# Linear attention and MLP, two layers: the third tile of the first MLP block turned by VectorE instead of TensorE

## The chip, the core and the metric

The kernel runs on one core of a Trainium2 chip. The time is the device time of one execution in microseconds (us). The kernel before takes 866.81 us, the median of three runs (866.64 to 866.84).

The engines are named as the profile names them: PE is TensorE (PEld its weight loads), DVE is VectorE, ACT is ScalarE, POOL is GpSimd. SPq and ACTq are the instruction queues of SyncE and ScalarE, from which DMA transfers are issued. A transfer is issued by one queue and lands later; whoever needs the data waits for the landing.

## What is computed

Two layers over x of 2048 rows by 448 columns in float32. Each layer adds a linear attention block (16 heads of 28 columns) to x, then an MLP block (448 to 1792 and back, gelu between), each on a layer norm of x:

```python
phi = lambda t: jnp.where(t > 0, t + 1, jnp.exp(t)) + 1e-6
pq, pk = phi(q), phi(k)
kv = jnp.einsum("bhsd,bhse->bhde", pk, v)
z = jnp.einsum("bhsd->bhd", pk)
num = jnp.einsum("bhqd,bhde->bhqe", pq, kv)
den = jnp.einsum("bhqd,bhd->bhq", pq, z)[..., None] + 1e-6
o = num / den
...
x = x + _A_ref(_layernorm(x, axis=-1), A_wqkv, A_wo)
x = x + _B_ref(_layernorm(x, axis=-1), B_w1, B_b1, B_w2, B_b2)
```

## The kernel before

**Tiles and stages.** The rows are cut into 16 tiles of 128 rows, and four tiles make a block. Per layer there are three stages. `phase1` goes over the 16 tiles: it makes k and the matrix G of the attention (and q for the first nine tiles). The middle, one pass over a list of tokens, turns G into the matrices M that stand for kv times the output weights, makes the queries that are left (tiles 9 to 15), and carries block 0 up to its MLP. The last stage runs the MLP over the four blocks; behind its matmuls it prepares the next block by a plan (`behind`).

**Precision.** A matmul operand is split into a high and a low part (hi by a cast on ScalarE, lo by a subtraction, mostly on VectorE), and a product is three matmuls: hi hi, hi lo, lo hi. `qh` and `ql`, `XH` and `XL` and `Mh` and `Ml` are such pairs.

**The middle.** It is written out by hand: `ORDER` (L605) is a string of tokens for each layer, and each token puts instructions at the end of the queues of the engines concerned. Every engine works through its own queue in order and waits where an operand isn't there. The tokens that matter here, j being one of the four tiles of block 0:

- `qz` (L810): GpSimd multiplies pq by z; `qs` (L814): VectorE sums that by head, takes the reciprocal and scales pq (L818 to L823); `tq` (L826): PE turns pq; `qq` (L835): ScalarE makes `qh` and VectorE `ql`; `o` (L845): twelve matmuls of `qh` and `ql` with M, in the order qh Mh, qh Ml, ql Mh (L850 to L852) for four groups.
- `la` (L867): VectorE adds the attention's output to x (L870), takes the statistics (L207, L219, L212), and GpSimd the power -1/2 (L213, `brs`); `lb` (L873): VectorE normalises the tile (L225, `xm`).
- `tu` (L296, for tiles 0 and 1): VectorE turns the tile in squares of 32 by 32 (L301, L302) into half of a 128 x 1024 square; `st` (L305) stores the square to DRAM from SP, `sp` (L309) loads it again in four transfers, so that the columns stand on the partitions; `x` (L887, by `split_t`) makes XH and XL of it.
- `T` (L883, for tiles 2 and 3): PE turns the tile with four transposes (L262); `x` (by `split_x`, L274 and L275) splits the result. For these tiles ScalarE first copies the last 64 columns once more behind the tile (L877).
- `Q`, `Qa`: eleven matmuls that make the queries of one tile (L337). `Qv` (L558) makes their phi with two passes of ScalarE and one of VectorE (L353, L354, L356) and stores it; `Qp` (L567) does it with three passes of ScalarE and an addition on GpSimd (L572 to L575).

After the list come the first matmuls of the MLP (L924, `hp`), which take all four tiles of XH side by side as their moving operand:

```python
MIDDLE = (
    "m0 qq1 m1 ms0 qq0 m2 ms1 m3 ms2 tq2 ms3 qz3 qs3 Qv1 o0 la0 qq2 o1 tq3 lb0 tu0 la1 qq3 Qv1 ",
    "m0 qq1 Qp m1 qz3 ms0 qq0 m2 ms1 m3 ms2 tq2 ms3 Qp qs3 o0 la0 qq2 o1 tq3 lb0 tu0 la1 qq3 ",
)
ORDER = [
    "Q ld1 ld0 ld2 G qz0 qz1 gt qs1 Q Qp kv qs0 tq1 Q mask qz2 tq0 qs2 ld3 b " + m +
    "o2 lb1 tu1 st la2 Q o3 sp Qv1 lb2 la3 Q T2 lb3 Qv1 x2 pre Qa x0 x1 T3 x3 Qa Qv "
    for m in MIDDLE
]
```

Of the kernel before, what the change touches and what calls it, by code (L numbers as in the profile page):

```python
# [9 lines left out]
F32 = mybir.dt.float32  # L10
# [12 lines left out]
def linear_attn_mlp_kernel(  # L23
# [12 lines left out]
    pe, act, dve, pool, sp = nc.tensor, nc.scalar, nc.vector, nc.gpsimd, nc.sync  # L36
    x0 = x_in[0]
# [7 lines left out]
    G = 112  # L45
# [10 lines left out]
    def dram(shape, dt, name):  # L56
        return tc.dram_tile(shape, dt, name=name)
# [15 lines left out]
    def t512(tag, bufs, name, dt=F32, at=0):  # L73
        n = 576 if tag in "BF" else 512
        return work.tile([128, n], dt, name=name, tag=tag, bufs=bufs)[:, at:at + 512]
# [217 lines left out]
    def half(name):  # L293
        return work.tile([128, 1024], F32, name=name, tag="S", bufs=5)
# [8 lines left out]
                      x[:, TL:].rearrange("p (m n) -> p m n", n=32)[:, None].to_broadcast([128, 2, 2, 32]))  # L303

    def store_sq(key, h):  # L305
        d = stored[key, h] = dram([128, 1024], F32, f"sq_{'_'.join(map(str, key))}_{h}")
        sp.dma_start(d, squares.pop((key, h)))

    def spread(key, h):  # L309
        r = spreads[key, h] = half("sp")  # L310
        d = stored.pop((key, h)).rearrange("(i r) (m f) -> m r i f", i=4, m=4)
        for m in range(4):
            sp.dma_start(r[m * 32:(m + 1) * 32].rearrange("r (i f) -> r i f", i=4), d[m])

    def split_t(key, t, hi, lo, eng=dve):

        x = spreads[key, t // 2].rearrange("p (i c u n) -> p u c i n", i=4, c=4, n=32)[:, t % 2]
        h = hi.rearrange("p (c i n) -> p c i n", c=4, n=32)
        act.copy(h, x)
        eng.tensor_tensor(lo.rearrange("p (c i n) -> p c i n", c=4, n=32), x, f(h), op=OP.subtract)  # L320
# [212 lines left out]
    def stage_q(l, t, cs=range(4), tag=None):  # L533
        if tag:
            qs_[l, t] = bank(tag, 4, "psq")[:, :D]
        qs_[l, t] = proj("q", ("a", l, t // 4), t % 4, qs_.get((l, t)), cs, q_at(l, t))
        if 3 in cs:
            qo.append((l, t, qs_.pop((l, t))))
# [16 lines left out]
            else:  # L555
                qo.append((0, t, o))

    def stage_qphi(n=9):  # L558
        for _ in qo[:n]:
            l, t, o = qo.pop(0)  # L560
            if (l, t) == (0, 0):
                by_rs(o)

            e = phi(o, "eq", tag="e" if t < NT - 2 else "E")
            sp.dma_start(pq_d[l][t * 128:(t + 1) * 128, :], e)

    def fill_qphi():  # L567

        l, t, o = qo.pop(0)
        e = t512("e", 3, "eq")[:, :D]  # L570
        p = t512("E", 2, "ep")[:, :D]
        act.activation(e, o, AF.Relu, scale=-1.0)  # L572
        act.activation(p, o, AF.Relu)
        act.activation(e, e, AF.Exp, scale=-1.0)
        pool.tensor_tensor(e, p, e, op=OP.add)  # L575
        sp.dma_start(pq_d[l][t * 128:(t + 1) * 128, :], e)

    def stage_g(l, t, acc, mid=lambda: None):
        h, lo = split.pop((l, t))
        kh, kl = ks.pop((l, t))  # L580
        first, last = t == 0, t == NT - 1
        x = [h[:, c * 128:(c + 1) * 128] for c in range(3)] + [h[:, TL:]]
        his = [(c, x[c], k) for c in range(4) for k in (kh, kl)]
        if t == NT - 3:
            his = his[::2] + his[1::2]
        los = [(c, lo[:, c * 128:(c + 1) * 128], kh) for c in range(3)]
        made = merge(his, los, g_at(l, t))
        for i, (c, w, k) in enumerate(made):
            if i == 3:
                mid()  # L590
            others = [m[0] for m in made[:i]], [m[0] for m in made[i + 1:]]
            pe.matmul(acc[c], w, k, start=first and c not in others[0], stop=last and c not in others[1])  # L592
# [5 lines left out]

    MIDDLE = (
        "m0 qq1 m1 ms0 qq0 m2 ms1 m3 ms2 tq2 ms3 qz3 qs3 Qv1 o0 la0 qq2 o1 tq3 lb0 tu0 la1 qq3 Qv1 ",
        "m0 qq1 Qp m1 qz3 ms0 qq0 m2 ms1 m3 ms2 tq2 ms3 Qp qs3 o0 la0 qq2 o1 tq3 lb0 tu0 la1 qq3 ",
    )
    ORDER = [  # L605
        "Q ld1 ld0 ld2 G qz0 qz1 gt qs1 Q Qp kv qs0 tq1 Q mask qz2 tq0 qs2 ld3 b " + m +
        "o2 lb1 tu1 st la2 Q o3 sp Qv1 lb2 la3 Q T2 lb3 Qv1 x2 pre Qa x0 x1 T3 x3 Qa Qv "
        for m in MIDDLE
    ]
    DEFER = NT - sum(tok in ("Q", "Qa") for tok in ORDER[0].split())  # L610

    STEP = "qp K T X s a kp n kh kl tu G bg Q ld sp"
# [260 lines left out]
    def o_n(l, b, j):  # L873
        t = b * 4 + j
        xn = xns["m", l, t] = ln_norm(sts.pop(("m", l, t)), f"xm{l}_{t}")
        if b == 0 and j >= 2:
            act.copy(xn[:, D:], xn[:, TL:D])  # L877

    def add_bias(l, b, j):
# [3 lines left out]
    def m_transpose(l, b, j):  # L883
        xn = xns.pop(("m", l, b * 4 + j))
        transpose_x(xn, xn[:, TL:], ("m", l, b), j)

    def m_split(l, b, j):  # L887

        if j < 2:
            split_t(("m", l, b), j, *block(("m", l, b)).pieces(j))  # L890
        else:
            split_x(("m", l, b), j)
# [175 lines left out]
    for l in range(LAYERS):  # L1068
        tr = SimpleNamespace(mp={})
        za, acc = phase1(l, tr)  # L1070
        if l == 0:
            background(0)
        fill = list(range(DEFER, NT))

        def biases(j):
            if l == 0:
                sp.dma_start(b1s, b1.rearrange("(c p) -> p c", p=128))
                sp.dma_start(b2b, b2[None, :].to_broadcast([128, D]))

        def pre(j):  # L1080
            for k in range(4):
                load_pq(l, 1, k)
            if l == 0:
                background(2)

        tok_ = SimpleNamespace(
            Q=lambda j: stage_q(l, fill.pop(0)), Qp=lambda j: fill_qphi(), Qv=lambda j: stage_qphi(j or 9),
            Qa=lambda j: stage_q(l, fill.pop(0), tag="acc"), G=lambda j: stage_g(l, NT - 1, acc, lambda: trans_z(tr, zs[l])),
            ld=lambda j: (load_pq(l, 0, j), load_x(l, j)), gt=lambda j: trans_gt(tr, acc),
            kv=lambda j: trans_kv(tr), mask=lambda j: trans_mask(tr), m=lambda j: trans_m(tr, j),  # L1090
            ms=lambda j: trans_ms(tr, j), qz=lambda j: q_z(l, 0, j, tr), qs=lambda j: q_scale(l, 0, j, tr),
            tq=lambda j: q_transpose(l, 0, j), qq=lambda j: q_split(l, 0, j), o=lambda j: o_mm(l, 0, j, tr),
            la=lambda j: o_ln(l, 0, j), lb=lambda j: o_n(l, 0, j), T=lambda j: m_transpose(l, 0, j),
            x=lambda j: m_split(l, 0, j), tu=lambda j: turn(xns.pop(("m", l, j)), ("m", l, 0), j),
            st=lambda j: store_sq(("m", l, 0), 0), sp=lambda j: spread(("m", l, 0), 0), pre=pre, b=biases)
        for tok in ORDER[l].split():
            name, j = tok.rstrip("0123456789"), int("0" + tok.lstrip("abcdefghijklmnopqrstuvwxyzQTG"))
            getattr(tok_, name)(j)
        assert not fill and not qo
        table(AF.Gelu_apprx_tanh)  # L1100
        q_z(l, 1, 0, tr)
        mlp1(l, 0, 0)
        trans_chunks(tr)
        for b in range(NB):
            acc = [bank("acc", 4, f"y{j}")[:, :D] for j in range(4)]
            nxt = b + 1 < NB
            if not nxt and l + 1 < LAYERS:
                st_k = stage_square(wqkv[:, D:2 * D])
                st_q = stage_square(wqkv[:, :D])
                load_to(l + 1, PRE - 1)  # L1110
            for i in range(NF):
                if i + 1 < NF:
                    mlp1(l, b, i + 1)
                elif nxt:
                    mlp1(l, b + 1, 0)
                if l == 0 and b == 0 and i:
                    background(1, 1)
                if i == NF - 2 and not nxt and l + 1 < LAYERS:
                    table(AF.Exp)
                if 9 <= i < 13:  # L1120
                    add_bias(l, b, i - 9)
                if nxt:
                    behind(l, b, i, tr)
                elif l + 1 < LAYERS:
                    if i == 2:
                        split_kq("k", st_k)
                    if i == 5:
                        split_kq("q", st_q)
                    if i in (3, 4, 6, 7, 8):
                        t = (3, 4, 6, 7, 8).index(i)  # L1130
                        stage_a(l + 1, t)
# [35 lines left out]
```

## Time and profile before

| | us |
|---|---|
| median of three runs | 866.81 |
| the profiled execution | 866.72 |
| its span, first to last instruction | 865.0 |
| busy in the span: PE, PEld, DVE | 860.0, 770.6, 494.6 |
| busy in the span: ACT, POOL | 346.5, 211.1 |

The span is 1.72 us shorter than the execution's time. The granted TensorE clock is full in all 40 slices of the page. Times in the views below are counted from the start of the span. The middle of layer 0 lies at about 104 to 135 us, that of layer 1 at about 530 to 561 us. A row of the timeline has the start, the time from first start to last end, the engine, the line, the operation with what it writes and reads, the shape, and how many such instructions follow each other.

### The profile page before, as it was taken

To read this page: it belongs to the slowest core of one execution; us is meant where nothing else is said; L and a number is where in the kernel's file an instruction comes from. 1 tells how busy PE (TensorE), PEld (TensorE's weight loads), DVE (VectorE), ACT (ScalarE), POOL (GpSimd) and SP (SyncE) were. 2 spreads that over 40 slices of the span, in tenths; PEclk is the share of its full clock that TensorE was granted. 3 is DMA by queue.
4 is the path that set the end of the run, shared out by engine and by line. 5 is a ranking of instruction groups with operands and counts; after the bars stand their busy time and mean duration, and the time that the engine had idled before them with its cause. 6 is when DMAs were issued, how large, how long until landed. Compare 5 with 4: busy or idle time off the path is not lost.

```text
span 865.0 us, 11662 instructions
## 1 busy us (share of the span) xinstructions
PE 860.0 (99%) x4181; PEld 770.6 (89%) x4181; DVE 494.6 (57%) x966; ACT 346.5 (40%) x606; POOL 211.1 (24%) x243
## 2 busy tenths in 40 slices
PE   9999999999999999999999999999999999999998
PEld 8999988888888888888899998988888888888887
DVE  7888596559456443236477876864674383533112
ACT  7776635333323322333356565433232233233231
POOL 3665612235013012012222343120220140140000
PEclk9999999999999999999999999999999999999999
DMA  5385536533313402051145433252332413111001
GB/s 171 128 248 174 183 90 216 183 112 108 134 61 117 147 0 98 1 182 49 49 152 185 163 130 108 103 187 80 117 109 88 139 72 112 50 49 43 0 1 43
DMA packets 63642, 94.76 MB, mean 110 GB/s; under 512 B 8928, under 2 KB 58720, under 8 KB 63584
## 3 DMA queue, kind: packets, MB, share of 16 engines
q1 hardware_dynamic: 63408, 93.87, 33.0%
q8 instruction: 33, 0.54, 0.3%
q14 instruction: 25, 0.20, 0.1%
q10 hardware_dynamic: 176, 0.14, 0.0%
HBM read 56.17 MB, written 34.60 MB: 105 GB/s over the span
## 4 chain that ended last, share of the span: by engine, by line
PE 99%; DVE 0%; issue 0%; ACT 0%; DVEq 0%
PE hp L924 32%; PE y L954 10%; PE y L953 10%; PE y L955 10%; PE G L592 8%; PE psq L337 8%; PE psk L337 8%; PE op L862 2%; PE op L861 2%; PE op L863 2%; PE op L851 1%; PE op L850 1%; PE op L852 1%; PE kvp L759 1%; PE mp L769 1%; PE psk L551 1%
## 5 line engine op out<-in xcount | busy, mean ns | idle before, releaser
L930 DVE TENSOR_TENSOR gl<-g,gh 128x512 fp32r<-128x512 f32 x112 | 83.2, 743 | 293.8 <-ACT gh L929 293.8
L926 ACT ACTIVATE g<-hp,b1s 128x512 f32<-128x512 f32 x112 | 77.4, 691 | 399.6 <-PE hp L924 398.8
L954 PE MATMUL y<-w2l,gh 128*128 128x448 f32 x447 | 163.6, 366 | 0.0
L953 PE MATMUL y<-w2h,gh 128*128 128x448 f32 x447 | 162.0, 362 | 0.0
L955 PE MATMUL y<-w2h,gl 128*128 128x448 f32 x447 | 160.1, 358 | 0.0
L924 PE MATMUL hp<-XH,w1h 128*128 128x512 f32 x336 | 130.7, 389 | 0.0
L924 PE MATMUL hp<-XH,w1l 128*128 128x512 f32 x336 | 130.7, 389 | 0.0
L924 PE MATMUL hp<-XL,w1h 128*128 128x512 f32 x336 | 130.1, 389 | 0.0
L213 POOL TENSOR_TENSOR brs<-bve,mhalf 128x1 f32<-128x1 f32 x63 | 39.3, 623 | 286.0 <-DVE bve L212 285.5
L953 PEld LDWEIGHTS y<-w2h,gh 128*128 128x128 f32 x447 | 83.7, 187 | 9.4
L954 PEld LDWEIGHTS y<-w2l,gh 128*128 128x128 f32 x447 | 83.9, 188 | 7.0
L955 PEld LDWEIGHTS y<-w2h,gl 128*128 128x128 f32 x447 | 84.0, 188 | 5.2 <-DVE gl L930 0.2
L924 PEld LDWEIGHTS hp<-XL,w1h 128*128 128x128 f32 x336 | 63.1, 188 | 13.1
L924 PEld LDWEIGHTS hp<-XH,w1h 128*128 128x128 f32 x336 | 63.0, 187 | 10.7
L924 PEld LDWEIGHTS hp<-XH,w1l 128*128 128x128 f32 x336 | 63.1, 188 | 9.9
L929 ACT CAST gh<-g 128x512 fp32r<-128x512 f32 x112 | 70.1, 626 | 3.5
L337 PE MATMUL psk<-wk,XH 128*128 128x448 f32 x210 | 61.8, 364 | 0.0
L337 PE MATMUL psq<-wq,XH 128*128 128x448 f32 x210 | 61.3, 366 | 0.0
L812 POOL TENSOR_TENSOR pz<-pq,zb 128x448 f32<-128x448 f32 x32 | 36.9, 1154 | 90.5 <-DVE dn L818 59.1
L462 POOL TENSOR_TENSOR xnl<-x,xnh 128x384 fp32r<-128x384 f32 x32 | 34.8, 1088 | 70.0 <-ACT xnh L461 56.7
L592 PE MATMUL G<-kh,xnh 128*128 128x448 f32 x128 | 46.8, 368 | 0.0
L592 PE MATMUL G<-kl,xnh 128*128 128x448 f32 x128 | 46.0, 365 | 0.0
(161 smaller groups left out, 1481.7 us busy)
## 6 DMA issues: line engine op xcount, KB each, us to landing
x<-in_A_x_dram SPq DMA_DIRECT2D x32, 224.0 KB, 3.7
pq_d<-eq SPq DMA_DIRECT2D x32, 224.0 KB, 2.7
pq<-pq_d SPq DMA_DIRECT2D x32, 224.0 KB, 3.2
sq_m<-sq SPq DMA_DIRECT2D x14, 512.0 KB, 2.8
sp<-sq_m SPq DMA_DIRECT2D x56, 128.0 KB, 2.8
x<-x_d SPq DMA_DIRECT2D x32, 224.0 KB, 3.5
sq_a<-sq SPq DMA_DIRECT2D x12, 512.0 KB, 2.9
sp<-sq_a SPq DMA_DIRECT2D x48, 128.0 KB, 2.8
```

What stands on the lines that cost most here:

```text
L213: pool.tensor_tensor(rs, ve, mhalf, op=OP.pow)
L337: pe.matmul(o, x, p, start=(i == 0), stop=(i == 10))
L462: pool.tensor_tensor(lo[:, :TL], xn[:, :TL], f(h[:, :TL]), op=OP.subtract)
L592: pe.matmul(acc[c], w, k, start=first and c not in others[0], stop=last and c not in others[1])
L812: pool.tensor_tensor(pz, pqt[l, b * 4 + j], tr.zb, op=OP.mult)
L924: pe.matmul(o, w, r, start=(k == 0), stop=(k == len(made) - 1))
L926: act.activation(g, hp, AF.Gelu_apprx_tanh, bias=b1s[:, i:i + 1])
L929: act.copy(gh, g)
L930: dve.tensor_sub(gl, g, f(gh))
L953: pe.matmul(acc[j], gh[:, s], w2h[:, i], start=first, stop=False)
L954: pe.matmul(acc[j], gh[:, s], w2l[:, i], start=False, stop=False)
L955: pe.matmul(acc[j], gl[:, s], w2h[:, i], start=False, stop=stop)
```

## The change

- The third tile (j = 2) of block 0's layer norm is turned by VectorE too (`turn_one`), into a half square of 128 x 512 in a buffer of tag A; it is stored by a transfer of its own (`st1`) and loaded by four (`sp1`). Its four PE transposes (`T2`) and its copy of the last columns are gone.
- The loads of both squares (`sp0`, `sp1`) are issued by SP and ScalarE in turn, two each, and stand behind both stores.
- `qz1` comes ahead of `qz0`.
- In layer 0 the phi of tiles 10 and 11 goes from `Qv` to `Qp` (ScalarE and GpSimd), behind `qs3` and `qq2`; in layer 1, where these were `Qp` already, they move to the same places.
- The outputs `o2` and `o3` stand next to each other; the queries of tile 12, which stood between them, follow. `la1` and `qq3` come ahead of `tu0`.
- The phi of tiles 12 and 13 is made by `Qh` without its store; `Qw` stores both after `x3`.

```diff
     def store_sq(key, h):
-        d = stored[key, h] = dram([128, 1024], F32, f"sq_{'_'.join(map(str, key))}_{h}")
-        sp.dma_start(d, squares.pop((key, h)))
-
-    def spread(key, h):
-        r = spreads[key, h] = half("sp")
-        d = stored.pop((key, h)).rearrange("(i r) (m f) -> m r i f", i=4, m=4)
+        sq = squares.pop((key, h))
+        d = stored[key, h] = dram(list(sq.shape), F32, f"sq_{'_'.join(map(str, key))}_{h}")
+        sp.dma_start(d, sq)
+
+    def spread(key, h, queues=(sp,)):
+        d = stored.pop((key, h))
+        r = spreads[key, h] = half("sp") if d.shape[1] == 1024 else t512("A", 2, "sp")
+        d = d.rearrange("(i r) (m f) -> m r i f", i=4, m=4)
         for m in range(4):
-            sp.dma_start(r[m * 32:(m + 1) * 32].rearrange("r (i f) -> r i f", i=4), d[m])
+            eng = queues[m % len(queues)]
+            eng.dma_start(r[m * 32:(m + 1) * 32].rearrange("r (i f) -> r i f", i=4), d[m])
+
+    def turn_one(x, key):
+        sq = squares[key, 1] = t512("A", 2, "sq")
+        sq = sq.rearrange("p (m c n) -> p c m n", m=4, c=4, n=32)
+        dve.transpose(sq[:, :3], x[:, :TL].rearrange("p (c m n) -> p c m n", c=3, n=32))
+        dve.transpose(sq[:, 3].rearrange("p (u m) n -> p u m n", u=2),
+                      x[:, TL:D].rearrange("p (m n) -> p m n", n=32)[:, None].to_broadcast([128, 2, 2, 32]))
...
-    def stage_qphi(n=9):
+    held = []
+
+    def stage_qphi(n=9, hold=False):
...
-            sp.dma_start(pq_d[l][t * 128:(t + 1) * 128, :], e)
+            held.append((pq_d[l][t * 128:(t + 1) * 128, :], e))
+            if not hold:
+                store_held()
+
+    def store_held():
+        while held:
+            sp.dma_start(*held.pop(0))
...
-    MIDDLE = (
-        "m0 qq1 m1 ms0 qq0 m2 ms1 m3 ms2 tq2 ms3 qz3 qs3 Qv1 o0 la0 qq2 o1 tq3 lb0 tu0 la1 qq3 Qv1 ",
-        "m0 qq1 Qp m1 qz3 ms0 qq0 m2 ms1 m3 ms2 tq2 ms3 Qp qs3 o0 la0 qq2 o1 tq3 lb0 tu0 la1 qq3 ",
-    )
     ORDER = [
-        "Q ld1 ld0 ld2 G qz0 qz1 gt qs1 Q Qp kv qs0 tq1 Q mask qz2 tq0 qs2 ld3 b " + m +
-        "o2 lb1 tu1 st la2 Q o3 sp Qv1 lb2 la3 Q T2 lb3 Qv1 x2 pre Qa x0 x1 T3 x3 Qa Qv "
-        for m in MIDDLE
-    ]
+        "Q ld1 ld0 ld2 G qz1 qz0 gt qs1 Q Qp kv qs0 tq1 Q mask qz2 tq0 qs2 ld3 b "
+        "m0 qq1 m1 ms0 qq0 m2 ms1 m3 ms2 tq2 ms3 qz3 qs3 Qp o0 la0 qq2 Qp o1 tq3 lb0 la1 qq3 tu0 "
+        "o2 lb1 la2 tu1 st0 o3 lb2 tu2 st1 la3 Q Qh Q sp0 sp1 lb3 Qh Qa x0 x1 x2 T3 x3 Qw pre Qa Qv "
+    ] * LAYERS
...
-        if b == 0 and j >= 2:
+        if b == 0 and j == 3:
             act.copy(xn[:, D:], xn[:, TL:D])
...
-        if j < 2:
+        if j < 3:
             split_t(("m", l, b), j, *block(("m", l, b)).pieces(j))
```

More of the change, by code (lines that the diff above doesn't have):

```diff
@@ L305, in store_sq @@
     def store_sq(key, h):
-        d = stored[key, h] = dram([128, 1024], F32, f"sq_{'_'.join(map(str, key))}_{h}")
-        sp.dma_start(d, squares.pop((key, h)))
-    def spread(key, h):
-        r = spreads[key, h] = half("sp")
-        d = stored.pop((key, h)).rearrange("(i r) (m f) -> m r i f", i=4, m=4)
-        for m in range(4):
-            sp.dma_start(r[m * 32:(m + 1) * 32].rearrange("r (i f) -> r i f", i=4), d[m])
-    def split_t(key, t, hi, lo, eng=dve):
-        x = spreads[key, t // 2].rearrange("p (i c u n) -> p u c i n", i=4, c=4, n=32)[:, t % 2]
+        sq = squares.pop((key, h))
[5 more added lines that the diff above has]
+        d = d.rearrange("(i r) (m f) -> m r i f", i=4, m=4)
+        for m in range(4):
+            eng = queues[m % len(queues)]
[6 more added lines that the diff above has]
+                      x[:, TL:D].rearrange("p (m n) -> p m n", n=32)[:, None].to_broadcast([128, 2, 2, 32]))
+    def split_t(key, t, hi, lo, eng=dve):
+        x = spreads[key, t // 2]
+        if x.shape[1] == 512:
+            x = x.rearrange("p (i c n) -> p c i n", i=4, c=4)
+        else:
+            x = x.rearrange("p (i c u n) -> p u c i n", i=4, c=4, n=32)[:, t % 2]
         h = hi.rearrange("p (c i n) -> p c i n", c=4, n=32)
@@ L885, in m_transpose, with turn_xm @@
         transpose_x(xn, xn[:, TL:], ("m", l, b), j)
+    def turn_xm(l, j):
+        xn = xns.pop(("m", l, j))
+        if j < 2:
+            turn(xn, ("m", l, 0), j)
+        else:
+            turn_one(xn, ("m", l, 0))
     def m_split(l, b, j):
-        if j < 2:
+        if j < 3:
             split_t(("m", l, b), j, *block(("m", l, b)).pieces(j))
@@ L1087, in linear_attn_mlp_kernel @@
             Q=lambda j: stage_q(l, fill.pop(0)), Qp=lambda j: fill_qphi(), Qv=lambda j: stage_qphi(j or 9),
+            Qh=lambda j: stage_qphi(1, True), Qw=lambda j: store_held(),
             Qa=lambda j: stage_q(l, fill.pop(0), tag="acc"), G=lambda j: stage_g(l, NT - 1, acc, lambda: trans_z(tr, zs[l])),
@@ L1093, in linear_attn_mlp_kernel @@
             la=lambda j: o_ln(l, 0, j), lb=lambda j: o_n(l, 0, j), T=lambda j: m_transpose(l, 0, j),
-            x=lambda j: m_split(l, 0, j), tu=lambda j: turn(xns.pop(("m", l, j)), ("m", l, 0), j),
-            st=lambda j: store_sq(("m", l, 0), 0), sp=lambda j: spread(("m", l, 0), 0), pre=pre, b=biases)
+            x=lambda j: m_split(l, 0, j), tu=lambda j: turn_xm(l, j),
+            st=lambda j: store_sq(("m", l, 0), j), sp=lambda j: spread(("m", l, 0), j, (sp, act)), pre=pre, b=biases)
         for tok in ORDER[l].split():
```

## The prediction

> **What bounds the kernel now.** I read the page first, then PE's waits, then the two middles by stretch.
>
> ```profile
> PE 860.0 (99%) x4181; PEld 770.6 (89%) x4181; DVE 494.6 (57%) x966; ACT 346.5 (40%) x606; POOL 211.1 (24%) x243
> ...
> PE 99%; DVE 0%; issue 0%; ACT 0%; DVEq 0%
> ...
> PE warm L170 <- DVE one L164: 1.1, 1, 1.1
> PE psk L551 <- ACT wk L137: 0.3, 1, 0.3
> ...
> 108.00:135.14 27.14, 27.14 (x144) 23.84 (x143) 23.93 (x53) 11.25 (x23) 4.49 (x6) 1.00 0.36 108
> 533.50:560.63 27.13, 27.13 (x145) 23.70 (x143) 22.86 (x48) 12.09 (x26) 6.40 (x8) 1.00 0.29 100
> ```
>
> PE is busy for 860.0 of 865.0 us, the chain of waits is PE for 99% of the span, and the view of who waited for whom has 1.4 us for PE in all, at the launch. So the end moves by what the change takes from PE's queue and by every wait that it puts in front of PE. The last two rows are the middles of the two layers by stretch (time; busy time of PE, PEld, DVE, ACT, POOL; clock; DMA). PE has no gap there, and VectorE is busy for 23.9 of 27.1 us and 22.9 of 27.1 us, in a stage with few gaps. Whether PE keeps going is decided by how early VectorE delivers.
>
> **What is removed from PE.** `T2`, four transposes per layer.
>
> ```profile
> 129.41 0.57 PE L337 MATMUL psq<-wq,XL 128*128 128x448 f32 x2
> 129.82 0.60 PE L262 MATMUL tp<-ident,xm 128*128 128x128 f32 x4
> 130.18 0.45 PE L337 MATMUL psq<-wq,XL 128*128 128x448 f32 x1
> 130.46 0.57 PE L337 MATMUL psq<-wq,XH 128*128 128x448 f32 x2
> ...
> 438.22 2.21 PE psq L337 x11
> ```
>
> From 129.41 to 130.46 PE starts three matmuls and the four transposes in 1.05 us. Eleven such matmuls take 2.21 us, 0.20 each, so three are 0.60 and the transposes cost 0.45 us. This is on the path: -0.45 us per layer, -0.9 us in all. That is the whole of what can be gained; nothing else leaves PE's queue.
>
> **What is moved next to PE: `o3` behind `o2`.** PE weight loads carry the waits. I work in layer 1, because its middle had the GpSimd phi behind `qs3` already.
>
> ```profile
> 545.89 0.19 PEld L850 LDWEIGHTS op<-Mh,qh 112*128 112x128 f32 x1
> 546.31 0.19 PEld L852 LDWEIGHTS op<-Mh,ql 112*128 112x128 f32 x1
> 548.24 0.79 PEld L337 LDWEIGHTS psq<-wq,XH 128*128 128x128 f32 x4
> ...
> 545.58 0.68 DVE L840 TENSOR_TENSOR ql<-tq,qh 112x512 fp32r<-112x512 f32 x1
> 546.32 0.51 DVE L225 TENSOR_SCALAR xm<-x,bmv,brs 128x448 f32<-128x448 f32 x1
> 546.87 0.58 DVE L301 STREAM_TRANSPOSE sq<-xm 128x384 f32<-128x384 f32 x1
> ...
> 547.56 0.59 DVE L870 TENSOR_TENSOR x<-op,x 128x448 f32<-128x448 f32 x1
> ...
> 549.13 0.68 DVE L840 TENSOR_TENSOR ql<-tq,qh 112x512 fp32r<-112x512 f32 x1
> ```
>
> `ql` of tile 2 ends at 545.58 + 0.68 = 546.26, and `o2` loads it at 546.31: already tight. Behind `o2` come the queries of tile 12, whose weight load starts at 548.24, four in 0.79 us. With `o3` there instead, its third load, the first of `ql`, is due at 548.24 + 0.40 = 548.64. Before, `ql` of tile 3 ended at 549.13 + 0.68 = 549.81, harmless since `o3` came eleven matmuls later. Now it has to come 1.17 us earlier or PE stands, with all of PE's queue behind it.
>
> VectorE's queue in between is, in the changed program: `xm` of tile 0, then x of tile 1 with its statistics, then this `ql`; the two transposes of tile 0 (0.69 us from 546.87 to 547.56 in the present order) come after it. If `xm` takes its usual 0.51 us, the next starts 0.43 us after it (553.44 to 553.87, below), x of tile 1 at 546.75, and `ql` ends 0.81 us earlier than before, at 549.00: PE stands for 0.38 us with the wake-up of 0.02. But GpSimd now has an addition (`Qp`) queued right behind `brs`:
>
> ```profile
> 542.42 1.16 POOL L575 TENSOR_TENSOR eq<-ep,eq 128x448 f32<-128x448 f32 x1 [3.37 <-ACT eq L574]
> 542.71 1.34 DVE L823 SCALAR_TENSOR_TENSOR pq<-pq,rd 128x448 f32<-128x448 f32 x1
> 117.27 0.63 DVE L823 SCALAR_TENSOR_TENSOR pq<-pq,rd 128x448 f32<-128x448 f32 x1
> ...
> 414.84 0.55 POOL L213 TENSOR_TENSOR brs<-bve,mhalf 128x1 f32<-128x1 f32 x1 [4.34 <-DVE bve L212]
> 415.36 2.42 POOL L881 TENSOR_TENSOR x<-x,b2b 128x448 f32<-128x448 f32 x2
> 415.43 1.33 DVE L426 TENSOR_SCALAR x<-x,bmv,brs 128x448 f32<-128x448 f32 x1 [0.73 <-POOL brs L213]
> ```
>
> The first rows show a GpSimd addition holding VectorE's scaling of pq: 1.34 us in layer 1, where it ran just ahead, 0.63 in layer 0, where none ran. The last three are the situation that the change makes: `brs`, the next GpSimd addition 0.52 us after its start, the normalisation 0.07 us later still, and it takes 1.33 us in place of 0.51. ScalarE has the operands of tile 11's phi ready long before: the cast of `qh` for tile 2 and three passes come first, and `brs` of tile 0 starts later.
>
> ```profile
> 543.14 0.59 ACT L839 CAST qh<-tq 112x512 fp32r<-112x512 f32 x1 [0.80 <-PE op L851]
> 545.74 0.55 POOL L213 TENSOR_TENSOR brs<-bve,mhalf 128x1 f32<-128x1 f32 x1 [2.16 <-DVE bve L212]
> ```
>
> Three passes about as long as the cast end by 543.73 + 1.8 = 545.5, before `brs` at 545.74, which GpSimd's queue has ahead of the addition. I take the held value: `xm` takes 1.33, x of tile 1 starts at 547.56, just where it was, `ql` ends at 549.81, and PE stands for 549.84 - 548.64 = 1.20 us. Ends for the range: 0.38 (not held) and 1.20.
>
> The Trainium skill (SBUF — State Buffer, Who interferes with whom) says that the second of two such operations is blocked for the whole of the first. By it the normalisation at 415.43 would have begun when the first of the two additions ended, 415.36 + 1.21 = 416.57, and taken 1.65 us. The row has 1.33, so the ends overlap; the sum goes by the row, and what the rule would make of it is the last rival.
>
> Layer 0 comes to the same. There the addition behind `qs3` is new and stretches the scaling from 0.63 to 1.34 us (+0.71), while a vector pass of phi behind it, about as long, goes; VectorE's queue then stands as it does in layer 1.
>
> **What is added at the end of the stage.** Tile 2 reaches PE over DRAM now.
>
> ```profile
> 551.13 0.58 DVE L870 TENSOR_TENSOR x<-op,x 128x448 f32<-128x448 f32 x1
> 553.44 0.51 DVE L225 TENSOR_SCALAR xm<-x,bmv,brs 128x448 f32<-128x448 f32 x1
> 553.87 0.62 DVE L870 TENSOR_TENSOR x<-op,x 128x448 f32<-128x448 f32 x1
> 551.23 0.32 SPq L307 DMA_DIRECT2D sq_m<-sq  x1
> 553.90 1.74 SPq L313 DMA_DIRECT2D sp<-sq_m  x4
> 861.77 0.38 ACTq L950 DMA_DIRECT2D out_dram<-x  x1
> 558.50 1.14 ACT L319 CAST XH<-sp 128x512 fp32r<-128x512 f32 x2
> 559.55 0.58 ACT L274 CAST XH<-tp 128x512 fp32r<-128x512 f32 x1
> 560.43 0.19 PEld L924 LDWEIGHTS hp<-XH,w1h 128*128 128x128 f32 x1
> 134.29 0.58 ACT L274 CAST XH<-tp 128x512 fp32r<-128x512 f32 x1
> 134.95 0.19 PEld L924 LDWEIGHTS hp<-XH,w1h 128*128 128x128 f32 x1
> ...
> x_d<-x SPq DMA_DIRECT2D x16, 224.0 KB, 2.0
> DMA to landing us min/median/max: 2.5/2.8/4.4
> ```
>
> The first MLP load stands at 560.43 and the last cast of XH ends at 560.13: 0.30 us to spare. (In layer 0 the cast ended at 134.87 with the load at 134.95.) With -0.45 and +1.20 PE comes there at 561.18.
>
> VectorE after `ql` at 549.13: `tu0` 0.60 later, 0.69 us; `xm` of tile 1, 0.43; so x of tile 2 starts at 550.85 (551.13 before). Statistics to 552.42 (1.57, as from 547.56 to 549.13), `tu1` to 553.12, `xm` of tile 2, `tu2` ending at 554.52. The first store goes at 553.24 and lands 2.67 us later (551.23 to 553.90 above), 555.91. The second, 256 KB, goes at 554.54; 224 KB took 2.0 us, 512 KB 2.67, so it lands at 556.6 to 557.2; I take 556.6. ScalarE's queue waits for both landings, and behind them stand the tail copy of tile 3, the phi of tile 13 and all casts of XH. Eight loads at 0.4 to 0.5 us, four on each queue (SP took 1.74 for four, ScalarE 0.38 for one): `sp0` is issued by 556.4, `sp1` by 557.3 (or 557.9). At 2.8 us they land at 559.2 and 560.1 (560.7). Casts of tiles 0 and 1, 0.51 each, from 559.2; tile 2 at 560.2; tile 3 ends at 561.3, 0.1 us behind PE's 561.18. With the late ends: 561.8, +0.6. With earlier landings 0. I take +0.1.
>
> **At no cost.** `qz1` first lets `qs1` start one GpSimd product earlier, but PE waits for nothing there, and VectorE's next input from PE (the mask's) isn't earlier. The removed copy frees ScalarE ahead of its wait for the landings. The two extra ScalarE passes of layer 0 stand in its gaps, 0.80 us ahead of the cast at 543.14. The held stores are read again only for later blocks, and SP's queue has the loads of the next block behind them. If such a cover were gone, each would cost at most its own length, about 0.6 us.
>
> **Sum.** Per layer -0.45 + 1.20 + 0.1 = +0.85, two layers +1.7. The profiled execution took 866.72 us (its span 865.0 and 1.72 around it), 0.09 under the median: 866.72 + 1.7 = 868.4 us, +0.18% on 866.81. A change under 0.2% (1.73 us) is what a measurement here can't tell from none, so 865.08 to 868.54 counts as the same.
>
> **Rivals.**
> - VectorE isn't held (the other side, not slower). If the GpSimd addition comes after `xm` of tile 0 has started, PE stands 0.38 us and VectorE is 0.8 us earlier at the end: -0.45 + 0.38 per layer, 866.6 us; with no wait of PE at all, -0.9, 865.8 us. It decides from 0.07 us, the lead of the addition over `xm` at 415. For it: the lead is that short. Against: with that very lead it held at 415.43. 17%.
> - The square comes late. The landings ranged from 2.5 to 4.4 us; with the loads from two queues at once a last landing half-way to 4.4, 3.6 us, brings tile 2 at 560.9 and the last cast at 562.0, 0.9 us behind PE: 866.72 + 2 x 1.65 = 870.0 us. For it: ScalarE's casts now stand behind two landings in a row. Against: the four loads of 553.90 met little other traffic. 21%.
> - VectorE is held until the addition has ended: 0.3 us more per layer (1.65 in place of 1.33), 869.0 us. Against it stands the row at 415.43. 5%.
>
> **How the numbers follow.** The forecast has 57%, its own range 867.8 to 869.2, from the end wait of 0 to 0.6 per layer less small errors in the stall. A third of that lies over 868.54: 0.21, with the late square 0.21 and the whole hold 0.04 that is 0.46 slower. Same: 0.36, 0.15 of the first rival and 0.01 of the last, 0.52. Faster would need -1.73, twice what leaves PE's queue: 0.02, for what I haven't seen. The range leaves out the best case and the worst landings: 866.0 to 870.3.
>
> **What would show it.** PE's waits would have two new entries, PE `op` (its third line) for VectorE's `ql` with 1.2 us each; `xm` of tile 0 would take 1.3 us in both layers with a GpSimd `eq` starting 0.07 us ahead; the first `hp` would wait up to some tenths for ScalarE's XH. `xm` at 0.5 us in both layers, or `o3` without a wait, would make the forecast wrong; so would a first `hp` that waits over 0.6 us.

## The result, and the profile after

| | before | after |
|---|---|---|
| median of four runs, us | 866.83 (866.64 to 867.98) | 872.0 (871.33 to 872.3) |
| the profiled execution, us | 866.72 | 872.3 |
| its span, us | 865.0 | 870.6 |

The kernel is 0.57% slower: the ratio of the times is 1.0057, with a 95% interval of 1.0045 to 1.0069. That is 5.2 us where +1.7 was forecast, and outside the range of 866.0 to 870.3 us.

The page of the changed kernel and its view of who waited for whom (PE's rows; us in total, how often, the longest):

```profile
PE 860.0 (99%) x4173; PEld 769.3 (88%) x4173; DVE 500.4 (57%) x968; ACT 345.7 (40%) x606; POOL 213.5 (25%) x245
...
PE hp L949 <- ACT XH L274: 3.0, 2, 1.9
PE op L870 <- DVE ql L858: 1.9, 2, 0.9
PE warm L170 <- DVE one L164: 1.1, 1, 1.1
PE psk L565 <- ACT wk L137: 0.9, 1, 0.9
```

PE has eight instructions fewer and two new waits, each once per layer: the first MLP matmul `hp` for ScalarE's XH, and `op` of tile 3 for VectorE's `ql`. Both were named in the prediction. (These rows have the waits of the matmuls; those of the weight loads ahead of them, in the timeline below, are some 0.4 us longer.) The wait at the launch (`psk`) is 0.6 us longer than before; no edit touches the launch.

The two middles by stretch, up to the first load of `hp` (time; busy time of PE, PEld, DVE, ACT, POOL; clock; DMA share, GB/s):

```profile
108.33:137.53 29.20, 27.14 (x141) 23.10 (x139) 24.77 (x49) 11.56 (x24) 6.28 (x8) 1.00 0.44 127
536.08:565.99 29.91, 27.07 (x139) 23.02 (x138) 24.68 (x49) 11.55 (x24) 6.22 (x8) 1.00 0.39 119
```

PE stands for 2.06 and 2.84 us in a stretch that had no gap before. Now the timeline of layer 1 along the chain that ends at the first `hp`, the changed kernel:

```profile
543.17 0.19 PEld L868 LDWEIGHTS op<-Mh,qh 112*128 112x128 f32 x1
...
548.31 0.55 POOL L213 TENSOR_TENSOR brs<-bve,mhalf 128x1 f32<-128x1 f32 x1 [2.16 <-DVE bve L212]
548.83 1.16 POOL L597 TENSOR_TENSOR eq<-ep,eq 128x448 f32<-128x448 f32 x1
548.89 1.34 DVE L225 TENSOR_SCALAR xm<-x,bmv,brs 128x448 f32<-128x448 f32 x1
551.75 0.68 DVE L858 TENSOR_TENSOR ql<-tq,qh 112x512 fp32r<-112x512 f32 x1
552.49 0.19 PEld L870 LDWEIGHTS op<-Mh,ql 112*128 112x128 f32 x1 [1.30 <-DVE ql L858]
...
555.81 1.62 SPq L308 DMA_DIRECT2D sq_m<-sq  x2
558.45 1.75 SPq L316 DMA_DIRECT2D sp<-sq_m  x4
558.48 1.80 ACTq L316 DMA_DIRECT2D sp<-sq_m  x4
563.80 1.66 ACT L333 CAST XH<-sp 128x512 fp32r<-128x512 f32 x3 [2.18 <-DMA sp<-sq_m]
565.37 0.58 ACT L274 CAST XH<-tp 128x512 fp32r<-128x512 f32 x1
565.99 0.19 PEld L949 LDWEIGHTS hp<-XH,w1h 128*128 128x128 f32 x1 [2.29 <-ACT XH L274]
```

The upper part is as forecast: the GpSimd addition starts 0.06 us ahead of `xm`, `xm` takes 1.34 us, and PE waits 1.30 us for `ql`. The lower part isn't. ScalarE stands idle for 2.18 us until the first square has landed, more than 5 us after its first load was issued, and PE waits 2.29 us for the casts behind it.

The views of the tile `sp` in layer 1 give the issues (ns; first and last start in us) and the landings. First the kernel before, then the changed one:

```profile
L313 SPq DMA_DIRECT2D sp<-sq_m x4: 318/423/429, 553.9 to 555.2; - x4
DMA to landing us min/median/max: 2.5/2.8/2.9
```

```profile
L316 SPq DMA_DIRECT2D sp<-sq_m x4: 309/372/425, 558.5 to 559.8; - x4
L316 ACTq DMA_DIRECT2D sp<-sq_m x4: 342/409/453, 558.5 to 559.8; - x4
DMA to landing us min/median/max: 3.2/4.4/4.8
```

Before, each load took 2.5 to 2.9 us, the last one issued at 555.2; so the whole square of 512 KB was there 4.2 us after its first load was issued. After, the square's four loads go out within 0.4 us, and the whole square is there 5.2 us after the first. One row of the kernel before gives the frame:

```profile
540.59 0.19 PEld L850 LDWEIGHTS op<-Mh,qh 112*128 112x128 f32 x1
```

From here on times are counted from this first load of `op` of the layer (540.59 before, 543.17 after), which takes out what earlier stages add. The chain of layer 1:

| step, us after the first `op` | before | forecast | after |
|---|---|---|---|
| first store issued | 10.64 | 12.65 | 12.64 |
| first load of the first square issued | 13.31 | 15.3 | 15.28 |
| first square landed | 17.5 | 18.6 | 20.5 |
| first `hp` | 19.84 | 20.7 | 22.82 |

Layer 1 loses 2.98 us. In layer 0 the first `op` is at 115.15 before and 115.48 after, `hp` at 134.95 and 137.53: 2.25 us. With 0.33 us that the first `op` of layer 0 already comes later, that is 5.56 us, and the span grew by 5.6.

### The profile page after: what moved, and what is told of

Its sections match the earlier page's. It is cut to its first block, busy times and chain, and to the rows that moved or that the text cites. A ratio compares the mean times of both kernels' runs of the same rounds, so it can differ in the third digit from the quotient of the medians.

```text
span 870.6 us, 11660 instructions
## 1 busy us (share of the span) xinstructions
PE 860.0 (99%) x4173; PEld 769.3 (88%) x4173; DVE 500.4 (57%) x968; ACT 345.7 (40%) x606; POOL 213.5 (25%) x245
## 4 chain that ended last, share of the span: by engine, by line
PE 93%; DMA 2%; DVE 2%; issue 1%; ACT 1%; POOL 0%; ACTq 0%; SPq 0%; DVEq 0%; POOLq 0%
PE hp L949 32%; PE y L979 10%; PE y L978 10%; PE y L980 10%; PE G L614 8%; PE psk L351 8%; PE psq L351 6%; PE op L880 2%; PE op L879 2%; PE op L881 2%; DMA sp<-sq_m 1%; PE kvp L777 1%; DMA sq_m<-sq 1%; PE op L883 1%; PE op L882 1%
## 5 line engine op out<-in xcount | busy, mean ns | idle before, releaser
L334 DVE TENSOR_TENSOR XL<-sp,XH 128x512 fp32r<-128x512 f32 x54 | 45.2, 849 | 5.7 <-ACT XH L333 4.3
```

## The experiments

Each was timed in five rounds against the kernel before on the same chip, which took 866.78 to 866.95 us there (medians); the 872.0 us of the changed kernel are from its own timing, beside 866.83. Counted from the first `op` of the layer, `hp` is 19.80 and 19.84 us before, 22.05 and 22.82 after.

### One queue for the loads

```diff
-            st=lambda j: store_sq(("m", l, 0), j), sp=lambda j: spread(("m", l, 0), j, (sp, act)), pre=pre, b=biases)
+            st=lambda j: store_sq(("m", l, 0), j), sp=lambda j: spread(("m", l, 0), j, (sp,)), pre=pre, b=biases)
```

> Edit: both squares are loaded from SP alone, as the single square was before; all else as in the changed kernel (872.0 us). Theory A (volume: the last load of a square lands about 4.2 to 4.5 us after the first was issued, whichever queues issue them, since the 16 DMA engines carry the packets one after the other): the first square lands about where it did (135.0 to 135.3 in layer 0, 563.2 to 563.6 in layer 1), the second later, as SP issues its loads 0.9 us later (136.6 to 137.0), so the last cast of XH comes 0.2 to 0.5 us later: 872.4 to 873.0 us. Theory B (two queues at once slow each other): each load lands 2.8 us after its own issue as before, the second square by 136.2, the first by 134.9, the first hp 0.3 to 0.6 us earlier per layer: 870.8 to 871.4 us.

Measured: 870.9 us (870.73 to 871.48), ratio 1.0047 (1.0033 to 1.0061). `sp` in layer 1:

```profile
L316 SPq DMA_DIRECT2D sp<-sq_m x8: 309/428/432, 558.0 to 561.2; - x8
DMA to landing us min/median/max: 2.0/2.4/3.0
```

The eight loads now go out over 3.2 us, and yet all have landed 5.2 us after the first was issued, where two queues took 5.9. The first square is there after 4.1 us in place of 5.2. In layer 0 nothing changes: 4.4 in place of 4.5 for the first square, 5.5 in place of 5.4 for both, and `hp` stays where it was (22.1), while in layer 1 it comes 1.1 us earlier. The median lies in theory B's range, by one layer alone; the later second square of theory A didn't come. But 5.2 us is the longest that was seen: in three more kernels below that load both squares from two queues (the next three) the first square is there after 4.4 to 4.7 us in either layer, and in one more with one queue (the three edits together) after 4.2 and 4.3. So how the 1.1 us that the medians differ by fall on the two layers isn't settled. Two queues saved time at the issue and gained nothing at the landing.

### No addition behind `brs` of tile 0

```diff
-        "m0 qq1 m1 ms0 qq0 m2 ms1 m3 ms2 tq2 ms3 qz3 qs3 Qp o0 la0 qq2 Qp o1 tq3 lb0 la1 qq3 tu0 "
+        "m0 qq1 m1 ms0 qq0 m2 ms1 m3 ms2 tq2 ms3 qz3 qs3 Qp o0 la0 qq2 o1 tq3 lb0 la1 qq3 Qp tu0 "
```

> Edit: the GpSimd phi of tile 11 is queued behind ql of tile 3 instead of ahead of o1, so that no GpSimd addition stands behind brs of tile 0. Main theory: xm of tile 0 takes 0.51 us instead of 1.34 in both layers, ql of tile 3 ends 0.8 us earlier, PE waits about 0.45 us for it instead of 1.28, the first store goes 0.8 us earlier and with it the whole chain to the first hp: 0.8 us per layer, 870.4 us (870.0 to 870.8). Rival: the addition then holds another instruction of VectorE ahead of the first store by as much (x of tile 2, a transposition): ql is earlier, the store isn't, 872.0 us.

Measured: 871.06 us (870.2 to 872.57), ratio 1.0048 (1.0036 to 1.0061). PE's wait for `ql` is gone from its list. Layer 1, the normalisations of tiles 0 and 1 on VectorE, and then GpSimd:

```profile
548.70 0.51 DVE L225 TENSOR_SCALAR xm<-x,bmv,brs 128x448 f32<-128x448 f32 x1
...
552.01 0.80 DVE L225 TENSOR_SCALAR xm<-x,bmv,brs 128x448 f32<-128x448 f32 x1
```

```profile
551.41 1.15 POOL L597 TENSOR_TENSOR eq<-ep,eq 128x448 f32<-128x448 f32 x1
```

Tile 0 isn't held any more; tile 1 is, and takes 0.80 in place of 0.48 us. So of the 0.83 us gained 0.33 are lost again, the first store stands at 12.14 us in both layers in place of 12.64, and the median's 0.9 us is about these 0.5 per layer: between the two theories. In the two profiled executions `hp` comes 0.27 and 1.07 us earlier, since their landings differ too.

### The queries between `o2` and `o3` again

```diff
-        "o2 lb1 la2 tu1 st0 o3 lb2 tu2 st1 la3 Q Qh Q sp0 sp1 lb3 Qh Qa x0 x1 x2 T3 x3 Qw pre Qa Qv "
+        "o2 lb1 la2 tu1 st0 Q o3 lb2 tu2 st1 la3 Qh Q sp0 sp1 lb3 Qh Qa x0 x1 x2 T3 x3 Qw pre Qa Qv "
```

> Edit: the queries of one tile stand between o2 and o3 again. PE's wait for ql of tile 3 (1.28 us per layer) goes. Theory A (the first hp is set by the chain of the squares: VectorE, store, loads, casts; the waits of PE don't add up): PE arrives 1.28 us earlier and waits that much longer for XH: 872.0 us (871.6 to 872.4). Theory B (the sum of the prediction, PE's waits add up): 872.0 - 2 x 1.28 = 869.4 us.

Measured: 871.91 us (871.21 to 874.59), ratio 1.0063 (1.005 to 1.0075). PE's waits:

```profile
PE hp L949 <- ACT XH L274: 4.5, 2, 2.3
```

The wait for `ql` is gone and the wait for XH has grown from 3.0 to 4.5 us; the time is what it was. PE's wait at `o3` is real, and costs nothing: what ends the stage isn't PE's queue but the chain of VectorE, stores, loads and casts.

### The casts of tile 3 first

```diff
-        "o2 lb1 la2 tu1 st0 o3 lb2 tu2 st1 la3 Q Qh Q sp0 sp1 lb3 Qh Qa x0 x1 x2 T3 x3 Qw pre Qa Qv "
+        "o2 lb1 la2 tu1 st0 o3 lb2 tu2 st1 la3 Q Qh Q sp0 sp1 lb3 Qh Qa T3 x3 x0 x1 x2 Qw pre Qa Qv "
```

> Edit: the casts of tile 3, whose operand comes from PE, stand ahead of those of tiles 0 to 2 in ScalarE's and VectorE's queues. Theory A (the landing of the first square and the casts behind it set the first hp): ScalarE does this cast in its idle time before the landing, one cast less (0.53 us) lies behind it: 0.5 us per layer, 871.0 us (870.7 to 871.4). Theory B (the second square's landing sets it, or PE): no change, 872.0 us.

Measured: 871.08 us (870.3 to 871.72), ratio 1.0046 (1.0033 to 1.0058). ScalarE in layer 1:

```profile
561.20 0.59 ACT L274 CAST XH<-tp 128x512 fp32r<-128x512 f32 x1 [0.27 <-PE tp L262]
562.31 1.66 ACT L333 CAST XH<-sp 128x512 fp32r<-128x512 f32 x3 [0.52 <-DMA sp<-sq_m]
```

Theory A: the cast of tile 3 goes into the wait for the landing, and 0.9 us of the time go with it. The square's landing and the casts behind it are on the path.

### Tile 2 on PE again

```diff
-        "o2 lb1 la2 tu1 st0 o3 lb2 tu2 st1 la3 Q Qh Q sp0 sp1 lb3 Qh Qa x0 x1 x2 T3 x3 Qw pre Qa Qv "
+        "o2 lb1 la2 tu1 st0 o3 lb2 la3 Q Qh Q sp0 lb3 T2 Qh x2 Qa x0 x1 T3 x3 Qw pre Qa Qv "
...
-        if b == 0 and j == 3:
+        if b == 0 and j >= 2:
...
-        if j < 3:
+        if j < 2:
```

> Edit: tile 2 goes through PE again (its four transposes, its copy), the second square is gone; the order, the held phi stores and the two queues for the first square stay. It asks why the first square's last load lands 4.5 to 5.2 us after its first was issued. Theory A (the 512 KB take what they take; before, from one queue, 4.2 and 4.5 us): 4.2 to 4.5 us again with no second square beside it, the first hp about 21.4 us after the first op of its layer (before 19.8, changed 22.05 and 22.8): 869.5 to 870.2 us. Theory B (the second square's packets hold the first up, two queues by themselves are faster): it lands 3.2 to 3.6 us after, PE then waits for ql of tile 3 alone, 21.1 us, 869.0 to 869.6 us. Theory C (two queues at once are slow by themselves): 4.5 to 5.2 us as in the changed kernel, 870.2 to 871.2 us.

Measured: 870.21 us (869.97 to 870.73), ratio 1.0038 (1.0024 to 1.0051). `sp` in layer 1:

```profile
L316 ACTq DMA_DIRECT2D sp<-sq_m x2: 365/597/829, 557.2 to 557.6; - x2
L316 SPq DMA_DIRECT2D sp<-sq_m x2: 320/372/425, 557.3 to 557.7; - x2
DMA to landing us min/median/max: 3.3/3.6/4.2
```

With no second square beside it the first lands 4.2 us after its first load in layer 0 and 4.6 in layer 1 (one queue before: 4.2 in both layers, not 4.2 and 4.5 as the text above has it). This rules out theory B: although all four loads are out after 0.4 us, the square is there no sooner than from one queue. What each load is issued sooner, it takes longer to land. Between A and C it doesn't decide: layer 0 lies in A's landing range, layer 1 in C's, and the time on their border. With the second square beside it, it was 4.5 and 5.2. Without the half square 3.3 of the 5.2 us remain, so most of the loss isn't the transport of tile 2.

### The first store early

```diff
-        "o2 lb1 la2 tu1 st0 o3 lb2 tu2 st1 la3 Q Qh Q sp0 sp1 lb3 Qh Qa x0 x1 x2 T3 x3 Qw pre Qa Qv "
+        "o2 lb1 tu1 st0 la2 o3 lb2 tu2 sp0 st1 la3 Q Qh Q sp1 lb3 Qh Qa x0 x1 x2 T3 x3 Qw pre Qa Qv "
```

> Edit: tu1 and the first store come ahead of la2 (as before), and the first square's loads ahead of the second store. Theory: x of tile 2 with its statistics (1.57 us of VectorE) stood in front of the first store, so it goes 1.57 us earlier (11.1 us after the first op in place of 12.65), its loads land 1.3 to 1.6 us earlier, and the second square, 0.7 us later than now, decides with two casts behind it: 0.7 to 1.5 us earlier per layer, 869.0 to 870.6 us. Rival (what decides is the second square alone): 872.0 to 873.0 us.

Measured: 873.36 us (872.82 to 873.65), ratio 1.0071 (1.0059 to 1.0084). The first store does stand at 11.15 us, and the first square lands at 18.2 in place of 19.75 (layer 0). ScalarE's queue, the same layer, and PE's waits:

```profile
128.69 0.85 ACTq L316 DMA_DIRECT2D sp<-sq_m  x2
...
133.69 0.84 ACTq L316 DMA_DIRECT2D sp<-sq_m  x2
134.57 0.24 ACT L895 COPY xm<-xm 128x64 f32<-128x64 f32 x1 [3.83 <-DMA sq_m<-sq]
...
135.78 1.65 ACT L333 CAST XH<-sp 128x512 fp32r<-128x512 f32 x3
```

```profile
PE tp L262 <- ACT xm L895: 2.7, 2, 1.4
```

The gain is eaten by ScalarE's queue. It issues the second square's loads, so it waits for the second store to land, which now lies behind the first square's loads and takes 4.0 us in place of 2.0; and behind this wait stand the tail copy of tile 3, which PE waits for, and the casts of a square that has been there for 2.7 us. Neither theory had this, and the time lies outside both ranges.

### Three edits together

One queue, no addition behind `brs` of tile 0, the casts of tile 3 first: the three diffs above.

> Edit: the three single edits together (loads from SP alone; no GpSimd addition behind brs of tile 0; the casts of tile 3 first). If the three act on one chain one after the other, the first hp comes about 20.9 us after the first op: about 1.1 us per layer over the kernel before, 869.1 us (868.6 to 869.7). If they cover each other, no better than the best of them alone, 870.9 us.

Measured: 869.1 us (868.86 to 869.6), ratio 1.0025 (1.0016 to 1.0035). One after the other on one chain: 1.1 + 0.94 + 0.92 is 2.96 us, and 872.0 - 2.96 is 869.04. `hp` stands 21.03 and 20.8 us after the first `op`. The first square, from one queue, is there 4.3 and 4.2 us after its first load.

### Everything on the chain moved

```diff
-        "m0 qq1 m1 ms0 qq0 m2 ms1 m3 ms2 tq2 ms3 qz3 qs3 Qp o0 la0 qq2 Qp o1 tq3 lb0 la1 qq3 tu0 "
-        "o2 lb1 la2 tu1 st0 o3 lb2 tu2 st1 la3 Q Qh Q sp0 sp1 lb3 Qh Qa x0 x1 x2 T3 x3 Qw pre Qa Qv "
+        "m0 qq1 m1 ms0 qq0 m2 ms1 m3 ms2 tq2 ms3 qz3 qs3 Qp o0 la0 qq2 o1 tq3 lb0 tu0 la1 qq3 Qp "
+        "o2 lb1 tu1 st0 la2 Q o3 sp0 lb2 tu2 st1 la3 Qh Q sp1 lb3 Qh Qa x0 x1 T3 x3 x2 Qw pre Qa Qv "
```

> Edit: everything on that chain moved: no addition behind brs of tile 0, tu0, tu1 and the first store early as before, the queries of a tile between o2 and o3, the first square loaded from SP, the second stored from ScalarE's queue and loaded from both, its casts last. If the chain from VectorE over the stores and loads is the whole cause, the first store goes about 10.3 us after the first op, the second about 13.8, its loads land at 19.0, and the first hp comes at 19.7, where it was before: 866.9 us (866.2 to 868.0). If something else in the change costs time (the queries' phi on GpSimd, the held stores, the exchange of the z products), it stays above 869 us.

Measured: 873.87 us (872.99 to 875.04), ratio 1.008 (1.0066 to 1.0093). PE's waits:

```profile
PE tp L262 <- ACT xm L895: 2.9, 2, 1.9
PE tp L262 <- DVE xm L225: 1.7, 2, 0.9
```

It fails as the kernel with the early store did: ScalarE waits for the second store, which takes 3.1 and 4.1 us beside the loads, and PE waits for the copy behind it. And tile 1's normalisation is held now (1.34 us). It doesn't tell whether the rest of the change costs time; the last three runs do.

### The kernel before with `la2` ahead of the store

```diff
-        "o2 lb1 tu1 st la2 Q o3 sp Qv1 lb2 la3 Q T2 lb3 Qv1 x2 pre Qa x0 x1 T3 x3 Qa Qv "
+        "o2 lb1 la2 tu1 st Q o3 sp Qv1 lb2 la3 Q T2 lb3 Qv1 x2 pre Qa x0 x1 T3 x3 Qa Qv "
```

> Edit in the kernel before: la2 (x of tile 2 with its statistics, 1.57 us of VectorE) ahead of tu1 and the store, as the change has it; nothing else of the change. Theory (the chain over the first store has 0.1 to 0.3 us to spare): the first store goes 1.57 us later, the first hp 1.3 to 1.5 us later per layer, 869.6 us (869.2 to 870.0). Rival (the store's time is covered): 866.9 us.

Measured: 872.22 us (870.81 to 872.79), ratio 1.0061 (1.0048 to 1.0073): as slow as the whole change. The first store stands 1.47 us later in both layers, `hp` 1.14 us later in layer 0 as expected, but 2.69 in layer 1. There the last of four loads landed late; the DMA queues of that stretch show what else ran:

```profile
DMA to landing us min/median/max: 2.5/2.8/4.7
```

```profile
q1 hardware_dynamic: 879, 1.01, 61.4%
q8 instruction: 1, 0.02, 1.3%
```

One load of instructions went through one of the 16 engines among the square's packets. Whether it is the cause of the 4.7 us wasn't tested, and it can't be the only cause of such a landing: in the last kernel of this section a load of a square took 4.2 us with no load of instructions beside it. Another 0.96 us of the profiled execution lie ahead of the first `op` (at 116.11).

So 1.14 us, in the layer with no such landing, is what the trace shows for `la2`, a little under what was expected. The time isn't explained by it: twice 1.14 us would be 869.2, and the five runs took 870.81 to 872.79. All of them lost at least 3.9 us, so what comes on top isn't chance of one execution, and its cause stays open.

### The rest of the change, with and without the hold

The kernel before with the exchange of the z products, the phi of tiles 10 and 11 by `Qp` at the changed places and the held stores; in the second run the second `Qp` stands behind `qq3`.

```diff
-    "m0 qq1 m1 ms0 qq0 m2 ms1 m3 ms2 tq2 ms3 qz3 qs3 Qv1 o0 la0 qq2 o1 tq3 lb0 tu0 la1 qq3 Qv1 ",
+        "m0 qq1 m1 ms0 qq0 m2 ms1 m3 ms2 tq2 ms3 qz3 qs3 Qp o0 la0 qq2 Qp o1 tq3 lb0 tu0 la1 qq3 "
...
-        "o2 lb1 tu1 st la2 Q o3 sp Qv1 lb2 la3 Q T2 lb3 Qv1 x2 pre Qa x0 x1 T3 x3 Qa Qv "
+        "o2 lb1 tu1 st0 la2 Q o3 sp0 Qh lb2 la3 Q T2 lb3 Qh x2 pre Qa x0 x1 T3 x3 Qw Qa Qv "
```

> Edit: of the change only the rest: the exchange of the z products, the phi of tiles 10 and 11 on ScalarE and GpSimd at the changed places in both layers, the held phi stores. Order of tu0, tu1, the stores and outputs, the loads from SP and T2 on PE are as in the kernel before. Theory: the GpSimd addition behind brs of tile 0 holds VectorE for 0.83 us ahead of the first store, of which 0.1 to 0.3 is covered: 0.5 to 0.7 us per layer, 868.1 us (867.8 to 868.4). Rival (these edits are at no cost where there is no wait for ql): 866.9 us; if one of the others costs something, over 868.5 us.

> Edit: the same rest of the change, with the second GpSimd phi behind qq3, so that no addition stands behind brs of tile 0. Theory: the phi's place is the only cost in this rest; the addition then holds tile 1's normalisation by 0.3 us, of which most is covered: 866.9 to 867.3 us. Rival (the exchange, the held stores or the phi's engine cost time by themselves): over 867.8 us.

Measured: 868.55 us (868.18 to 869.15), ratio 1.0019 (1.001 to 1.0028), and 868.49 us (868.22 to 869.21), ratio 1.002 (1.0012 to 1.0029). The first lost what was expected, `hp` 0.68 and 0.56 us later; its median lies 0.15 us over the range, and in its profiled execution the first `op` comes 0.49 us later. The second isn't: moving the addition gained nothing. Its layer 1, GpSimd, then VectorE:

```profile
550.65 0.55 POOL L213 TENSOR_TENSOR brs<-bve,mhalf 128x1 f32<-128x1 f32 x1 [3.01 <-DVE bve L212]
551.17 1.15 POOL L597 TENSOR_TENSOR eq<-ep,eq 128x448 f32<-128x448 f32 x1
```

```profile
547.68 0.51 DVE L225 TENSOR_SCALAR xm<-x,bmv,brs 128x448 f32<-128x448 f32 x1
...
551.23 1.34 DVE L225 TENSOR_SCALAR xm<-x,bmv,brs 128x448 f32<-128x448 f32 x1
```

The addition now stands behind `brs` of tile 1, and holds tile 1's normalisation by the same 0.83 us. The first store is as late in one as in the other, 11.45 us. One move of the change is in none of these kernels: `pre`, the loads of the next block, stands behind `Qw` in the changed kernel. It wasn't tested alone.

### The exchange and the held stores alone

The same kernel with the phi of tiles 10 and 11 where they were before (`Qv1` in layer 0, `Qp` in layer 1).

> Edit: of the change only the exchange of the z products and the held phi stores; the phi of tiles 10 and 11, the order, the loads and T2 as in the kernel before. Theory (what the last two kernels lost is the GpSimd addition that holds VectorE ahead of the first store, behind brs of tile 0 or of tile 1): normalisations of 0.51 us, first store 10.6 to 10.9 us after the first op, 866.9 us (866.6 to 867.4). Rival (the exchange or the held stores cost it): 868.0 us or more.

Measured: 867.14 us (866.69 to 867.68), ratio 1.0003 (0.9994 to 1.0012): no difference that the interval can tell, up to 0.12% (1.0 us). The first store is back at 10.82 and 10.62 us, and `hp` in layer 1 at 19.82. In the profiled execution `hp` of layer 0 is 0.96 us later all the same, since the last of the square's four loads took 4.2 us (before 2.9):

```profile
DMA to landing us min/median/max: 2.4/2.8/4.2
```

With the phi stores held, SP issues the next block's loads 3.6 us earlier in this layer, right behind the square's (130.34 in place of 133.95). In layer 1 they stand as close, and the last load took 2.9 us, so their nearness alone doesn't make it late. By the medians these two edits cost little or nothing; what the two kernels before it lost comes with the phi's place (in layer 0 also with its engines, since `Qv` made it before).

## Why the prediction was wrong

**Right, by its own rows.** What leaves PE is four transposes per layer (x4173 after x4181). VectorE is held at `xm` of tile 0 (1.34 us in both layers against 1.33 forecast), `ql` ends late, and PE's third load of `o3` waits for 1.30 us against 1.20. The first rival (VectorE not held) fell with the same rows. So did the last, the hold to the very end of the addition: `xm` would have ended 0.51 us after the addition, at 550.50, and ended at 550.23. The first store was forecast 2.0 us later and was.

**The step that failed** is in the part on the end of the stage: "`sp0` is issued by 556.4", "At 2.8 us they land at 559.2". That is 18.6 us after the first `op`; it landed at 20.5. The 2.8 us was read from loads that one queue issued 0.4 us apart, and applied to loads that two queues issue within 0.4 us. But the four loads of a square share the 16 DMA engines, which were busy for 0.91 of the time in the middle of the square's landing in the kernel before (the last two numbers of the row are their busy share and the GB/s; a phi store of 224 KB, issued at 555.74, is in it too):

```profile
556.00:557.00 1.00, 1.00 (x7) 0.92 (x6) 0.51 (x1) 0.17 (x2) 0.24 (x1) 1.00 0.91 283
```

With four loads out at once (tile 2 on PE) the square lands 4.2 and 4.6 us after its first load, where one queue before took 4.2 in both layers; the time in which the queue issues isn't what a landing waits for. The chain of the kernel before was in the trace: store 2.0 us later, the same 2.7 to the first load, the same 4.2 to the landing, and four casts in 2.1 put the last cast's end 21.5 to 21.7 us after the first `op`, an end wait of about 1 us per layer, and 870.2 to 870.5 us in all. With the second square beside the first, from two queues, the landing came another 0.3 (layer 0) and 1.0 us (layer 1) later in this execution, and 0.2 to 0.5 in three other kernels with these loads. So the term "+0.1" with its late end of +0.6 measured 1.4 and 2.1 us: `hp` at 22.05 and 22.82, where PE would have been at 19.8 - 0.45 + 1.30 = 20.7.

The rival that the square comes late had the mechanism, at 21%, but on the wrong square and with its size from the same wrong start: it let the last load of tile 2 land at 3.6 us behind its issue. That one took 4.0 and 4.6, but ScalarE was still at the casts of the first square then; what it waited for was the first square, whose last load took 4.05 and 4.8. The argument against it, "the four loads of 553.90 met little other traffic", misses that the four meet each other, and the phi store behind them: 2.8 us a load held for loads that went out 0.4 us apart. (Two slips there are without weight: 562.0 is 0.8 us behind 561.18, not 0.9, and a third of 57% is 0.19, not 0.21.)

The Trainium skill (DMA: Bandwidth & Descriptors, Issuing engines are not separate DMA queues) states that transfers from different engines run on the same 16 DMA engines and that issuing from several saves only the time of issuing. The trace agrees: 4.2 to 4.6 us from two queues, 4.2 from one; with the second square two queues took 4.4 to 5.2 us in four kernels, one queue 4.1 to 4.4 in two.

**The wait at `o3` was sized well and is no term.** With the queries between `o2` and `o3` again, PE waits 1.5 us longer at `hp` over both layers and the time stays. The prediction had PE at 561.18 and the casts at 561.3, a near tie, and so took the wait for what sets the end. With the square's chain 2 us behind, the hold of VectorE costs by delaying the first store, not by stopping PE.

**"At no cost"** holds for the exchange and the held stores as far as the medians tell (867.14 us). The phi's place costs about 0.6 us per layer through the first store, a path on which the forecast put nothing. What the forecast didn't price is the order on VectorE: `la2` in front of `tu1` puts x of tile 2 and its statistics, 1.57 us, ahead of the first store. It was in its timetable, and its price vanished in the shortened landing. Alone in the kernel before, it costs 1.14 us in layer 0, and the kernel 5.3 us in all; most of that stays open. So the split of the 5.2 us among `la2`, the phi's place and the landing isn't settled, though each moved the time of kernels that differ in it: by 5.3 us, by 1.6, and by 1.1 from two queues to one.

No version here beats the kernel before. The best with the half square is 869.1 us. Its second square is then what ScalarE's last cast waits for in layer 0 (0.14 us), in layer 1 it lands just as the cast before it ends; and the transposes that it saves are 0.45 us per layer.

## What to carry to other kernels

Read a transfer's time from the first issue to the last landing of the whole group, not from one load's issue to its landing: issuing the group faster only moved the time from the queue into the landing here. When an engine's queue also issues transfers, everything behind the issue waits for what the transfer waits for, so put the copies and casts that others need ahead of it. And before pricing PE's waits, find the chain that ends last at the stage's end: a wait on an engine that would wait later anyway was free here, while vector work ahead of a store was paid for the most part (0.6 us of 0.8, and 1.14 of 1.47 in layer 0).

## What the runs showed of the hardware

- VectorE's normalisation ends 0.24 to 0.25 us after a GpSimd addition that it meets, whatever its start: 550.23 after 549.99 (started 0.06 us behind it), 552.81 after 552.56 (0.60 us behind), 552.57 after 552.32 (0.06). It takes 0.51 us alone, so by these records the two overlap for the addition's last 0.26 us. The Trainium skill (SBUF — State Buffer, Who interferes with whom) has the second one blocked for the whole of the first; the rows have it nearly so.
- A store of 256 KB took 2.0 us to land with little beside it and 4.0 us behind four loads of 128 KB.
- The last of a square's four loads from one queue, with no second square, took 2.9 to 3.3 us in eight of ten landings (the kernel before and the last four kernels), 4.2 and 4.7 in the other two.
- The first `op` of layer 0 came between 114.9 and 116.1 us in these kernels. Between the kernel before and the one with `la2` ahead, which have the same instructions up to there, the difference is 0.96 us, as much as most single edits here are worth.
